# w_out by seven products in batches 1 and 2, squares summed by transfers, and the forms of W held or fetched in smaller pieces

## The chip, the cores and the metric

The kernel runs on one core of a Trainium2 chip. The metric is device time in microseconds of one launch, taken as the median of several runs; lower is better. Engines are named as in the profile: PE (TensorE matmuls), PEld (its weight loads), DVE (VectorE), ACT (ScalarE), POOL (GpSimd) and SP (the queue of SyncE, which only issues transfers here).

## The reference

Channel attention over four batches of 6080 tokens with 256 channels, followed by a feed-forward layer with a squared relu. All arrays are float32.

```python
qn = q / (norm(q, axis=1) + 1e-6); kn = k / (norm(k, axis=1) + 1e-6)   # q, k, v: (4, 6080, 256)
a = softmax(kn.transpose(0, 2, 1) @ qn / tau)                          # 256 x 256 for each batch
x = (v @ a).reshape(24320, 256)
h = maximum(x @ w_in, 0)                                               # w_in: 256 x 2048
out = (h * h) @ w_out                                                  # w_out: 2048 x 256
```

## The kernel before

The kernel folds the attention matrix into w_in: for each batch it makes W = a @ w_in once, so that the feed-forward layer reads v directly. Every float32 product is made of three matmuls on rounded parts (hi by hi, hi by lo, lo by hi). Both products of the layer are done by Strassen-like schemes in which 2 x 2 blocks of the operands take seven block products in place of eight.

The tokens of a batch are cut into 12 blocks: ten of 512 and two of 480. Two blocks of batch 0 come first in a plain way; from block 2 of batch 0 on, work goes by periods. A period k has a batch b, a block n and a group j of 512 hidden units (j = 0 to 3), four periods to a block, 180 in all. The function `period` writes a period's instructions by hand, and the engines keep this order.

In a period PE makes the seven products of v by the forms of W (named A11, S1, S2, A12, S4, S3, A22 in the order of their use; three matmuls by two halves each, 42 in all, 256 columns wide or 240 in the short blocks), and, for the periods one and two back, the products with w_out: `window_A`, `window_S(.., "S1")` and `window_S(.., "S2")`. A group holds two pairs of hidden blocks. A period is called plain (function `plain`) if only its first pair goes by seven products with w_out and the second by eight. A plain period has 39 of these matmuls, of which three (in the S2 window) are twice as wide: 512 columns, 480 in the short blocks. A period that is not plain has 42, all of 256 or 240 columns. Before the change j = 0 and j = 1 are plain in batches 0, 1 and 2, and no period of batch 3 is; j = 2 and 3 are not plain from block 3 of batch 0 on.

After a product ACT and DVE take its sums out of PSUM, square them (relu on DVE in `relu_squares`, or on ACT where `FREE` holds), make sums of the squares (`first_sums`, `third_sum`, `last_sum`) and split them into hi and lo (`hi_A`, `lo_A`, `hi_S`, `lo_S`). Where a period is plain, the sums and the A parts cover one pair in place of two.

Beside this, `attention` works on the next batch, stepped by `side` at five points of a period: one chunk of q and k per period, which costs 12 matmuls for the Gram matrix, a split on ACT and DVE, a square on ACT and the sum of the squares (`add_squares`) into the tile `acc` on DVE. When its 25 chunks are done, the norms, the softmax and W follow, and `late_forms` makes the forms of W and writes them to DRAM (`wf_kept`). From there `load_forms` fetches them for each period again, four transfers of 384 or 512 KB through SP: the early forms (A11, S1, S2) two periods ahead, the late ones (A12, A22, S3, S4) one ahead. SP's queue is in order: a transfer that waits holds up those behind it. POOL's queue carries the loads of v, the sums of the outputs (`combine`, by accumulating transfers) and their stores.

## Time and profile before

| what | value |
|---|---|
| median of 3 runs | 2139.14 us (2138.82 to 2139.2) |
| span of the profiled execution | 2137.0 us, so about 2.1 us of the median lie around it |
| PE busy | 2123.9 us, 99% of the span |
| DVE busy | 1947.1 us, 91% |
| ACT busy | 1818.6 us, 85% |
| products of the periods on PE | from 160 us to 2083 us |

A matmul's record covers its whole way through the array, so records overlap; what a matmul costs is read from the distance between two starts, and a wait of PE from the idle time ahead of a row.

### The profile page before, as it was taken

The page shows a single profiled execution, that of the slowest core. Times are in us where ns is not written, and L with a number is a line of the kernel's source. Part 1 is how long each engine was busy: PE and PEld are TensorE (multiplying, and loading weights), DVE is VectorE, ACT ScalarE, POOL GpSimd, SP SyncE. Part 2 cuts the span into 40 slices and gives each one's busy share as a digit, 9 for nine tenths or more (in the row PEclk, how much of TensorE's full clock was granted, in tenths as well). Part 3 has the DMA queues.
Part 4 walks back from the last instruction along what each step waited for, and adds up shares of the span by engine and source line. Part 5 has one row for each costly group of instructions (what it writes and reads, how often), then busy time and mean ns, then how long its engine had stood idle before and what let it go on. Part 6 is the DMA issues. An engine that isn't in the chain of part 4 may idle for free.

```text
span 2137.0 us, 43905 instructions
## 1 busy us (share of the span) xinstructions
PE 2123.9 (99%) x16990; PEld 2066.1 (97%) x16990; DVE 1947.1 (91%) x2577; ACT 1818.6 (85%) x2708; POOL 403.4 (19%) x506
## 2 busy tenths in 40 slices
PE   9999999999999999999999999999999999999999
PEld 8789999999999999999999999999999999999998
DVE  6898999998999999988999999999899999999993
ACT  5887888888888888878888888878888999999995
POOL 0000121211222121221222121121212122122121
PEclk9999999999999999999999999999999999999999
DMA  9777888889998888788999788887999788788783
GB/s 345 234 232 264 240 255 252 235 239 283 303 297 262 251 251 262 234 241 247 292 303 288 248 255 257 249 234 229 325 322 314 233 241 252 220 247 248 233 256 86
DMA packets 258865, 548.24 MB, mean 257 GB/s; under 512 B 26848, under 2 KB 120672, under 8 KB 258656
## 3 DMA queue, kind: packets, MB, share of 16 engines
q1 hardware_dynamic: 193696, 449.32, 62.3%
q0 software_dynamic: 64960, 96.11, 20.9%
q8 instruction: 134, 2.20, 0.4%
q14 instruction: 75, 0.61, 0.1%
HBM read 431.75 MB, written 64.23 MB: 232 GB/s over the span
## 4 chain that ended last, share of the span: by engine, by line
PE 89%; DVE 6%; ACT 2%; DMA 2%; issue 1%; SPq 0%; DVEq 0%; ACTq 0%
PE ps_o L27 41%; PE ps_c L27 16%; PE ps_h L27 14%; PE ps_b L27 11%; PE gram L27 4%; DVE x L27 2%; PE ps_w L27 2%; PE ps_o_m L27 1%; ACT x L27 1%; DMA wf<-wf_kept 1%; DVE s_lo L27 1%; DVE acc L27 1%; DMA qk<-in_k 1%; DVE A_lo L27 0%; DMA qk<-in_q 0%
## 5 line engine op out<-in xcount | busy, mean ns | idle before, releaser
L27 DVE TENSOR_TENSOR s_lo<-x,s_hi 128x1024 fp32r<-128x1024 f32 (+1 forms) x384 | 464.0, 1208 | 44.4 <-ACT s_hi L27 44.1
L27 PE MATMUL ps_c<-v_hi,wf 128*128 128x256 f32 (+1 forms) x2160 | 466.9, 280 | 4.4 <-DVE x L27 2.2
L27 POOL DMA_DIRECT2D o<-o x225 | 245.4, 1253 | 1102.7 <-ACT o L27 689.7
L27 ACT CAST s_hi<-x 128x1024 fp32r<-128x1024 f32 (+1 forms) x384 | 399.7, 1041 | 37.6 <-DVE x L27 27.9
L27 DVE TENSOR_TENSOR x<-x 128x1024 f32<-128x1024 f32 (+3 forms) x540 | 389.6, 722 | 10.3
L27 PEld LDWEIGHTS ps_c<-v_hi,wf 128*128 128x128 f32 x2160 | 367.4, 188 | 7.8 <-ACT ps_c L27 3.3
L27 ACT ACTIVATE x<-x 128x512 f32<-128x512 f32 (+2 forms) x540 | 350.0, 648 | 21.7 <-DVE x L27 9.2
L27 PE MATMUL ps_b<-v_hi,wf 128*128 128x256 f32 (+1 forms) x1440 | 309.7, 279 | 1.8 <-DVE nx L27 1.1
L27 PE MATMUL ps_h<-v_hi,wf 128*128 128x256 f32 (+1 forms) x1440 | 309.1, 278 | 0.0
L27 PE MATMUL ps_c<-v_lo,wf 128*128 128x256 f32 (+1 forms) x1080 | 300.9, 279 | 0.0
L27 DVE TENSOR_TENSOR A_lo<-x,A_hi 128x1024 fp32r<-128x1024 f32 (+3 forms) x360 | 276.9, 792 | 18.8 <-ACT A_hi L27 15.3
L27 ACT CAST A_hi<-x 128x1024 fp32r<-128x1024 f32 (+3 forms) x360 | 254.4, 707 | 38.4 <-DVE x L27 25.5
L27 PEld LDWEIGHTS ps_b<-v_hi,wf 128*128 128x128 f32 x1440 | 245.2, 188 | 2.3 <-DVE nx L27 1.3
L27 PEld LDWEIGHTS ps_h<-v_hi,wf 128*128 128x128 f32 x1440 | 244.9, 188 | 0.0
L27 ACT COPY x<-ps_c 128x512 f32<-128x512 f32 (+1 forms) x180 | 105.1, 584 | 158.3 <-PE ps_c L27 158.0
L27 PEld LDWEIGHTS ps_c<-v_lo,wf 128*128 128x128 f32 x1080 | 203.2, 188 | 0.1
L27 PE MATMUL ps_b<-v_lo,wf 128*128 128x256 f32 (+1 forms) x720 | 200.6, 279 | 0.0
L27 PE MATMUL ps_h<-v_lo,wf 128*128 128x256 f32 (+1 forms) x720 | 200.4, 278 | 0.0
L27 DVE TENSOR_TENSOR x<-x,ps_h 128x512 f32<-128x512 f32 (+1 forms) x180 | 122.4, 680 | 76.9 <-PE ps_h L27 76.6
L27 PE MATMUL ps_o<-s_hi,wo_hi 128*128 128x256 f32 (+3 forms) x954 | 190.1, 295 | 0.5 <-ACT s_hi L27 0.5
L27 PE MATMUL ps_o<-s_hi,wo_lo 128*128 128x256 f32 (+3 forms) x954 | 190.2, 295 | 0.0
L27 PE MATMUL ps_o<-s_lo,wo_hi 128*128 128x256 f32 (+3 forms) x954 | 190.0, 295 | 0.1
(166 smaller groups left out, 5166.9 us busy)
## 6 DMA issues: line engine op xcount, KB each, us to landing
wf<-wf_kept SPq DMA_DIRECT2D x360, 512.0 KB, 5.3
wf<-wf_kept SPq DMA_DIRECT2D x360, 384.0 KB, 4.9
o<-o POOLq DMA_DIRECT2D x114, 256.0 KB, 5.9
qk<-in_k SPq DMA_DIRECT2D x87, 256.0 KB, 4.3
qk<-in_q SPq DMA_DIRECT2D x87, 256.0 KB, 4.8
v<-in_vT POOLq DMA_DIRECT2D x76, 256.0 KB, 5.1
out_T<-o POOLq DMA_DIRECT2D x152, 128.0 KB, 4.7
o<-o POOLq DMA_DIRECT2D x76, 128.0 KB, 6.2
```

The source lines that it names most:

```text
L27: return lambda *args, **kwargs: self.tc.keep_in_program_order(issue(*args, **kwargs))
```

## The change

1. `FROM`, which says up to which block a group is plain, goes from all of batches 0, 1 and 2 to blocks 0 to 9 (j = 0) and 0 to 8 (j = 1) of batch 0 alone. 53 periods stop being plain: two and three in batch 0, 24 each in batches 1 and 2.
2. In batches 2 and 3 the squares of q and k are added into `acc` by accumulating transfers on POOL's queue, 24 for a batch; the next chunk is then loaded one period later, and the end of the attention waits one period more.
3. The early forms of a group get a tile of their own (`w_own0` to `w_own3`) and are fetched once a batch, 768 KB in one transfer; the late ones come as four transfers of 256 KB through a ring of four tiles, each issued behind the product that frees its slot.
4. `AFTER_FROM` and `V_LAST_FROM` give batches 1 and 2 the order of parts that batch 3 has; `FREE_FROM` moves a relu from DVE to ACT from block 7 of these batches on.

```diff
-                if self.b == 1 and c < HEAD:
+                if self.b > 1 or self.b == 1 and c < HEAD:
                     pool_engine.dma_start(a, sq, accum_op=ALU.add)
                 else:
                     vector.tensor_add(a, a, sq)
...
             g.add_squares(c)
+            c -= b > 1
             if c0 <= c and c + ahead < g.n:
                 load(c + ahead)
...
-    AFTER_FROM = (12, 12, 12, 0)
-    FREE_FROM = (12, 12, 12, 0)
+    AFTER_FROM = (12, 0, 0, 0)
+    FREE_FROM = (12, 7, 7, 0)
...
-    FROM = {0: (12, 12, 12, 0), 1: (12, 12, 12, 0)}
+    FROM = {0: (10, 0, 0, 0), 1: (9, 0, 0, 0)}
...
+    def load_early(k):
+
+        if k >= len(groups):
+            return
+        b, n, j = groups[k]
+        assert (b, j) in forms_kept
+        if k >= GPB and groups[k - GPB][0] == b:
+            WF[k, 0] = WF[k - GPB, 0]
+            return
+        own = own_tile(j, 3 * 2 * 2 * P, F32R, f"wf{k}_own")
+        WF[k, 0] = own.rearrange("p (i r s m) -> p i r s m", i=2, r=2, s=3)
+        nc.sync.dma_start(WF[k, 0].bitcast(F32), wf_early[b, j])
...
+            f = form[0]
+            t = ring_tile([P, 2, 2, P], f"wf{k}_{f}")
+            WF[k, f] = t.rearrange("p i r (s m) -> p i r s m", s=1)
+            nc.sync.dma_start(t.bitcast(F32), wf_later[b, j, f])
...
-        load_forms(k + 2, 0)
+        load_early(k + 2)
...
         product(k, B2, A12, B21)
+        load_late(k + 1, A12)
...
-        steps = V_LAST if b == B - 1 else V_STEPS
+        steps = V_LAST if b >= V_LAST_FROM else V_STEPS
```

The place where the change is widest is the S2 window. On PE, in the period of batch 1, block 3, j = 3, stands the window for j = 1 two periods back (ps_o are the output sums, s_hi and s_lo the parts of the squares, wo and wS the weights and their sums). Before, one of its three terms reads:

```order
L27 MATMUL ps_o_3_1_9313<-s_hi_9412,wS_hi 128x256
L27 MATMUL ps_o_3_1_9313<-s_hi_9412,wo_hi 128x256
L27 MATMUL ps_o_3_0_9283<-s_hi_9412,wo_hi 128x512
L27 MATMUL ps_o_3_0_9283<-s_hi_9412,wo_hi 128x256
L27 MATMUL ps_o_3_1_9313<-s_hi_9412,wo_hi 128x256
```

In the changed kernel two of the three terms of the same window read:

```order
L27 MATMUL ps_o_3_1_9366<-s_hi_9458,wS_hi 128x256
L27 MATMUL ps_o_3_1_9366<-s_hi_9458,wS_odd_hi 128x256
L27 MATMUL ps_o_3_1_9366<-s_hi_9458,wo_hi 128x256 x2
L27 MATMUL ps_o_3_1_9366<-s_hi_9458,wS_lo 128x256
L27 MATMUL ps_o_3_1_9366<-s_hi_9458,wS_odd_lo 128x256
L27 MATMUL ps_o_3_1_9366<-s_hi_9458,wo_lo 128x256 x2
```

Each term has lost its wide matmul here and four of 256 columns are left; the other windows of the group gain what makes the count of matmuls the same. Over the program 123 matmuls of 512 columns have become 256 wide, and 36 of 480 have become 240 wide; the number of matmuls is as before.

On DVE, in the period of batch 1, block 2, j = 2, while chunk 7 of batch 2 is worked on (x are the squares of a period, qk a chunk, v the next block of tokens), before:

```order
L27 TENSOR_TENSOR s_lo_8788<-x_8595,s_hi_8787 128x1024
L27 SCALAR_TENSOR_TENSOR x_8747<-x_8747 128x2x512
L27 TENSOR_TENSOR s_lo_8808<-x_8595,s_hi_8807 128x1024
L27 TENSOR_TENSOR acc_7752<-acc_7752,qk_7_8402 128x1024
L27 TENSOR_TENSOR v_lo_3_8676<-v_3_8241,v_hi_3_8675 128x768
L27 TENSOR_TENSOR A_lo_8839<-x_8747,A_hi_8838 128x2x512
```

and in the changed kernel:

```order
L27 TENSOR_TENSOR s_lo_8829<-x_8640,s_hi_8828 128x1024
L27 SCALAR_TENSOR_TENSOR x_8791<-x_8791 128x2x512
L27 TENSOR_TENSOR s_lo_8854<-x_8640,s_hi_8853 128x1024
L27 TENSOR_TENSOR v_lo_3_8798<-v_3_8349,v_hi_3_8797 128x1024
L27 TENSOR_TENSOR A_lo_8894<-x_8791,A_hi_8893 128x2x512
```

The addition into `acc` has left DVE for POOL's queue, and the parts of v come one step later in the block.

On SP, where batch 1 ends and batch 2 begins (the sums of W for j = 3 of batch 2 are written, and the next periods' forms are fetched), before:

```order
L27 DMA wf_kept_3_0_3_165<-wS_hi_3_14076 256x1x256
L27 DMA wf_kept_3_0_4_166<-wS_hi_3_14076 256x1x256
L27 DMA wf_kept_3_1_3_167<-wS_lo_3_14077 256x1x256
L27 DMA wf_kept_3_1_4_168<-wS_lo_3_14077 256x1x256
L421 DMA qk_1_14224<-in_q 128x512
L983 DMA wf_0_0_14182<-wf_kept_1_0_3_157 128x768
L983 DMA wf_0_1_14184<-wf_kept_1_1_3_159 128x768
```

and in the changed kernel:

```order
L27 DMA wf_early_3_132<-wS_hi_3_14302 128x2x256
L27 DMA wf_later_3_3_183<-wS_hi_3_14302 128x2x128
L27 DMA wf_later_3_2_182<-wS_hi_3_14302 128x2x128
L27 DMA wf_early_3_132<-wS_lo_3_14303 128x2x256
L27 DMA wf_later_3_3_183<-wS_lo_3_14303 128x2x128
L27 DMA wf_later_3_2_182<-wS_lo_3_14303 128x2x128
L1004 DMA wf_own<-wf_early_3_132 128x1536
L1013 DMA wf_1_14405<-wf_later_1_1_173 128x512
```

The fetch of the early forms of j = 3 (`wf_own`) now stands right behind the writes of the same array, and the fetch of A12 for j = 1 (`wf_1`, for the next period) behind it. Before, a fetch of other forms stood there, and that of j = 3 came eight transfers later.

## Rows read from the trace of the kernel before

**Rows 1.** The page: the span, and busy time, share and instructions of PE and DVE.

```profile
span 2137.0 us, 43905 instructions
PE 2123.9 (99%) x16990; PEld 2066.1 (97%) x16990; DVE 1947.1 (91%) x2577; ACT 1818.6 (85%) x2708; POOL 403.4 (19%) x506
```

**Rows 2.** Busy time in four stretches: batch 1 with the attention beside it (12 periods, blocks 3 to 5), batch 1 with W and its forms beside it (20 periods, blocks 7 to 11), the same 20 periods of batch 2, and batch 3 with nothing beside it (20 periods). Columns: stretch, its length, then busy time and instructions of PE, PEld, DVE, ACT and POOL, the granted clock as a share of 2.4 GHz, the share of the DMA engines, and GB/s.

```profile
735.29:871.93 136.64, 136.64 (x1155) 135.85 (x1154) 131.42 (x162) 120.58 (x175) 26.92 (x33) 1.00 0.83 255
915.46:1127.97 212.51, 211.34 (x1752) 207.50 (x1751) 192.73 (x279) 174.91 (x273) 43.04 (x52) 1.00 0.89 271
...
1443.79:1653.97 210.18, 209.54 (x1735) 205.73 (x1734) 191.12 (x269) 174.79 (x274) 44.20 (x55) 1.00 0.94 297
1693.11:1890.57 197.46, 197.46 (x1682) 197.08 (x1682) 186.43 (x231) 184.05 (x282) 39.52 (x50) 1.00 0.79 238
```

**Rows 3.** What PE waited for from 160 us to the end: total us, times, longest us.

```profile
PE ps_c L27 <- DVE x L27: 2.2, 5, 0.9
PE ps_c L27 <- ACT ps_c L27: 2.1, 3, 0.9
PE ps_b L27 <- DVE nx L27: 1.1, 1, 1.1
PE ps_b L27 <- DMA wf<-wf_kept: 0.7, 1, 0.7
```

**Rows 4.** The order of time on PE: start, length of the merged records, operation, count. Two pairs of 512 columns in the plain blocks; the first and the row behind the last of 12 matmuls of 256 columns; the first and the row behind the last of 18 of 240 columns; two pairs of 480 columns.

```profile
100.29 0.63 PE L27 MATMUL ps_h<-v_hi,w_lo 128*128 128x512 f32 x2
100.76 0.63 PE L27 MATMUL ps_o<-s_hi,wo_hi 128*128 128x512 f32 x2
...
788.64 0.28 PE L27 MATMUL ps_o<-s_hi,wS_hi 128*128 128x256 f32 x1
...
790.04 0.28 PE L27 MATMUL ps_b<-v_hi,wf 128*128 128x256 f32 x1
...
1640.15 0.39 PE L27 MATMUL ps_o<-s_hi,wS_hi 128*128 128x240 f32 x2
...
1642.16 0.28 PE L27 MATMUL ps_b<-v_hi,wf 128*128 128x240 f32 x1
...
2087.16 0.60 PE L27 MATMUL ps_h<-v_hi,w_hi 128*128 128x480 f32 x2
2087.59 0.60 PE L27 MATMUL ps_h<-v_lo,w_hi 128*128 128x480 f32 x2
```

**Rows 5.** DVE's groups by shape in the first stretch of Rows 2: count, busy us, mean ns of one, idle time ahead of them and what ended it.

```profile
L27 DVE TENSOR_TENSOR acc<-acc,qk 128x1024 f32<-128x1024 f32 x12 | 14.6, 1219 | 0.0
L27 DVE TENSOR_TENSOR x<-x 128x512 f32<-128x512 f32 x18 | 12.3, 685 | 0.0
L27 DVE SCALAR_TENSOR_TENSOR x<-x 128x1024 f32<-128x1024 f32 x9 | 11.0, 1219 | 0.0
L27 DVE TENSOR_TENSOR A_lo<-x,A_hi 128x512 fp32r<-128x512 f32 x12 | 8.2, 687 | 1.8 <-ACT A_hi L27 1.8
...
L27 DVE TENSOR_TENSOR A_lo<-x,A_hi 128x1024 fp32r<-128x1024 f32 x6 | 7.3, 1222 | 0.2
L27 DVE TENSOR_TENSOR x<-x 128x1024 f32<-128x1024 f32 x6 | 7.3, 1219 | 0.0
...
L27 DVE TENSOR_TENSOR x<-x 128x256 f32<-128x256 f32 x12 | 5.1, 422 | 0.2
```

**Rows 6.** ACT's groups by shape in the same stretch, same columns.

```profile
L27 ACT ACTIVATE x<-x 128x512 f32<-128x512 f32 x30 | 19.0, 634 | 0.8
...
L27 ACT CAST A_hi<-x 128x512 fp32r<-128x512 f32 x13 | 8.1, 625 | 1.7 <-PE ps_c L27 1.5
...
L27 ACT CAST A_hi<-x 128x1024 fp32r<-128x1024 f32 x6 | 6.3, 1052 | 0.0
...
L27 ACT CAST A_hi<-x 128x256 fp32r<-128x256 f32 x6 | 2.4, 407 | 0.2
```

**Rows 7.** What DVE waited for in the second stretch of Rows 2 (915.46 to 1127.97): the largest entry.

```profile
DVE x L27 <- PE ps_h L27: 15.0, 15, 2.4
```

**Rows 8.** The page's transfers: queue, count, KB each, median us from issue to landing.

```profile
wf<-wf_kept SPq DMA_DIRECT2D x360, 512.0 KB, 5.3
...
wf_kept<-wS_lo SPq DMA_DIRECT2D x24, 256.0 KB, 7.5
...
acc<-qk_heads POOLq DMA_DIRECT2D x3, 512.0 KB, 6.1
```

**Rows 9.** In order of time where batch 1 ends and batch 2 begins, start and length: the first matmul of the last period of batch 1 on PE, the last sums of W for batch 2 on DVE, and SP's merged issues.

```profile
1116.13 0.27 PE L27 MATMUL ps_b<-v_hi,wf 128*128 128x240 f32 x1
...
1116.40 1.22 DVE L27 TENSOR_TENSOR wS_lo<-w_sums,wS_hi 128x1024 fp32r<-128x1024 f32 x1
...
1119.63 1.34 SPq L27 DMA_DIRECT2D wf_kept<-wS_hi  x2
1121.01 2.87 SPq L27 DMA_DIRECT2D wf_kept<-wS_lo  x2
...
1124.69 16.47 SPq L983 DMA_DIRECT2D wf<-wf_kept  x10
```

**Rows 10.** DVE and PE in order of time at the norms of batch 2: start, length, count, and the idle time ahead with what ended it.

```profile
924.92 1.80 DVE L27 TENSOR_TENSOR v<-v 128x256 f32<-128x256 f32 x4
...
926.85 0.38 PE L27 MATMUL ps_b<-v_hi,wf 128*128 128x256 f32 x1 [1.11 <-DVE nx L27]
```

More of the change, by code (lines that the diff above doesn't have):

```diff
@@ L163 @@
     wi_kept = [[scratch.tile([P, NC, GRP], F32, name=f"wi_kept{g}_{i}") for i in range(2)] for g in range(NG)]
-    wf_kept = {
-        (b, g, i): [scratch.tile([P, 2, n, P], F32, name=f"wf_kept{b}_{g}_{i}_{n}") for n in (3, 4)]
+    wf_early = {(b, g): scratch.tile([P, 2, 2, 3, P], F32, name=f"wf_early{b}_{g}") for b in range(B) for g in range(NG)}
+    wf_later = {
+        (b, g, f): scratch.tile([P, 2, 2, P], F32, name=f"wf_later{b}_{g}_{f}")
         for b in range(B)
         for g in range(NG)
-        for i in range(2)
+        for f in range(1, 5)
     }
@@ L195, in keep_blocks @@
     def keep_blocks(b, g, i, part, issue):
-        early, later = wf_kept[b, g, i]
-        src = part.bitcast(F32).rearrange("p c (r i m) -> p c r i m", r=2, i=2)
-        for to, c, f in ((early[:, :, 0, :], 0, 0), (later[:, :, 0, :], 1, 0), (later[:, :, 1, :], 1, 1)):
-            issue(to, src[:, c, :, f, :])
+        src = lambda c, f: part(c).bitcast(F32).rearrange("p (r i m) -> p r i m", r=2, i=2)[:, :, f, :]
+        issue(wf_early[b, g][:, i, :, 0, :], src(0, 0))
+        issue(wf_later[b, g, A12[0]][:, i], src(1, 0))
+        issue(wf_later[b, g, A22[0]][:, i], src(1, 1))
     def keep_sums(b, g, i, part, issue):
-        early, later = wf_kept[b, g, i]
         src = part.bitcast(F32).rearrange("p (r s m) -> p r s m", r=2, s=4)
-        issue(early[:, :, 1:3, :], src[:, :, 0:2, :])
-        issue(later[:, :, 2:4, :], src[:, :, 2:4, :])
+        issue(wf_early[b, g][:, i, :, 1:3, :], src[:, :, 0:2, :])
+        for s, form in ((2, S3), (3, S4)):
+            issue(wf_later[b, g, form[0]][:, i], src[:, :, s, :])
+    by_half = lambda tile: lambda c: tile[:, c, :]
+    A11, S1, S2 = ((0, at) for at in range(3))
+    A12, S4, S3, A22 = ((1 + at, 0) for at in range(4))
     wp_kept = [[scratch.tile([P, NC, GRP], F32, name=f"wp_kept{g}_{i}") for i in range(2)] for g in range(NG)]
@@ L325, in forms_of_W @@
         w32, S = room()
-        vector.tensor_add(w32, w_hi.bitcast(F32), w_lo.bitcast(F32))
+        for c in range(NC):
+            vector.tensor_add(w32[:, c, :], w_hi(c).bitcast(F32), w_lo(c).bitcast(F32))
         yield
@@ L329, in forms_of_W @@
             keep_blocks(b, g, i, part, nc.sync.dma_start)
-        if b == B - 1:
-            for kept, part in zip(wp_kept[g], (w_hi, w_lo)):
-                nc.sync.dma_start(kept, part.bitcast(F32))
         w4, S4 = v(w32), S.rearrange("p (r s m) -> p r s m", r=2, s=4)
@@ L362, in late_forms @@
         for i, part in enumerate((w_hi, w_lo)):
-            keep_blocks(b, g, i, part, sync.dma_start)
+            keep_blocks(b, g, i, by_half(part), sync.dma_start)
         if b == B - 1:
@@ L392, with ring_tile, own_tile, W_tiles @@
     OWN_BUFS = {"qk": QK_BUFS, "dec": 1}
-    FAST_TAGS = ("qk",) * QK_BUFS + ("w_lo",) * NG + ("w_hi",) * NG
+    FAST_TAGS = ("qk",) * QK_BUFS + tuple(f"w_own{g}" for g in range(NG)) + ("s1_hi", "s1_lo", "s2_hi", "s2_lo")
+    def ring_tile(shape, name):
+        return wpool.tile(shape, F32R, tag="w_ring", name=name, bufs=4)
+    def own_tile(g, cols, dt, name):
+        return wpool.tile([P, 6, C], dt, tag=f"w_own{g}", name=name, bufs=1).rearrange("p a c -> p (a c)")[:, 0:cols]
+    def W_tiles(b, g):
+        own, more = own_tile(g, 3 * GRP, F32R, f"w{b}_{g}"), ring_tile([P, GRP], f"w_lo{b}_{g}")
+        return (lambda c: own[:, c * GRP : (c + 1) * GRP]), (lambda c: more if c else own[:, 2 * GRP : 3 * GRP])
     class Gram:
@@ L580, in attention @@
         yield
+        if b > 1:
+            yield from until("mid")
+            yield
         yield from until("dve")
@@ L771, in load_v_blocks @@
         half = tn // 2
-        raw = pool.tile([P, 8, half], F32, tag="v", name=f"v{b}_{n}", bufs=1)
+        raw = pool.tile([P, 7, half], F32, tag="v", name=f"v{b}_{n}", bufs=1)
         for slot, c in ((1, 1), (3, 0)):
@@ L861, in first_product @@
             tensor.matmul(
-                ps[:, :tn], wt[:, c, f0 : f0 + P], vt[:, c, :tn], start=i == 0, stop=i == len(parts) - 1
+                ps[:, :tn], wt(c)[:, f0 : f0 + P], vt[:, c, :tn], start=i == 0, stop=i == len(parts) - 1
             )
@@ L999, in two_halves @@
         return ps_h.tile([P, 2, T // 2], F32, tag=tag, name=name)
-    A11, S1, S2 = ((0, at) for at in range(3))
-    A12, A22, S3, S4 = ((1, at) for at in range(4))
     T3, B21, B22, B11, T1, T2, T4 = range(7)
@@ L1013, in product @@
         for p in range(2):
-            late, at = form
-            w_hi, w_lo = (WF[k, late, i][:, p, at, :] for i in range(2))
+            piece, at = form
+            w_hi, w_lo = (WF[k, piece][:, i, p, at, :] for i in range(2))
             for i, (wt, vt) in enumerate(((w_hi, v_hi), (w_hi, v_lo), (w_lo, v_hi))):
@@ L1329, in period @@
         product(k, C, A22, T4)
+        load_late(k + 1, A22)
         evict_C21(k)
@@ L1420 @@
         if i == 26:
-            load_forms(0, 0)
-            load_forms(0, 1)
+            load_early(0)
+            for form in (A12, S4, S3, A22):
+                load_late(0, form)
     for _ in prep:
```

46 lines of the change are left out of this document (22 added, 24 removed).

## The prediction, made before the changed kernel ran

> **What bounds the kernel now.** The page comes first: PE is busy for 2123.9 of the span's 2137.0 us, DVE for 91% [rows 1]. Since matmul records overlap, a busy PE proves little, so the next view is what PE waited for: from 160 us to the end 6.1 us in all, none of it regular [rows 3]. PE then runs its matmuls as closely as it can, and the price of one is the distance between starts: 0.465 us for two of 512 columns, 0.233 each; 12 of 256 columns in 1.40 us, 0.117 each; 18 of 240 in 2.01 us, 0.112 each; 0.43 us for two of 480, 0.215 each [rows 4]. The stretches confirm it: batch 3 has 1682 matmuls in 197.46 us, 0.117 us each [rows 2]. The clock is granted in full, the 2.4 GHz level, in all four stretches, so no term below changes it. The matmuls' columns bound the kernel; DVE is close behind, with 131.42 of 136.64 us (96%) beside the attention and 192.73 of 212.51 (91%) beside W and its forms [rows 2]. What is to be decided is whether fewer columns on PE are paid for by work on DVE, ACT and the queues that now takes the lead.
>
> **PE, removed.** 53 periods stop being plain, and in each three matmuls become half as wide, at an equal count: 123 go from 512 to 256 columns and 36 from 480 to 240. That is 123 x (0.233 - 0.117) = 14.3 us and 36 x (0.215 - 0.112) = 3.7 us [rows 4], **18.0 us** together. All of it lies on the engine that sets the end. Here a rule speaks against the change: the Trainium skill, "TensorE: Matmul & The Clock Gate", section "Back-to-back issue gap", says that in a stream of weight loads and matmuls the spacing is set by both, about 81 ns at 128 columns and 131 ns at 512; read straight between them this is an estimate of 98 ns at 256, 33 ns for a halved width, and 159 x 33 ns = 5 us in place of 18. The rows differ: 233 against 117 ns. Its case stands among the rivals.
>
> **DVE and ACT, added and removed.** A period that stops being plain sums two pairs instead of one. On DVE `first_sums` goes from 512 to 1024 elements (1.219 - 0.685), two further sums from 256 to 512 (2 x (0.685 - 0.422)), the early A parts from 512 to 1024 (1.222 - 0.687) and the late ones from 256 to 512 (about 0.26, from the sums of these sizes): 1.86 us [rows 5]. On ACT `hi_A` adds (1.052 - 0.625) + (0.625 - 0.407) = 0.64 us [rows 6]. Beside the attention of batches 1 and 2 a block of four periods gains 2 x 1.86 = 3.7 us on DVE and loses four additions into `acc`, 4 x 1.22 = 4.9 us [rows 5]. DVE goes from 131.42 / 3 = 43.8 to 42.6 us a block, PE from 45.5 to 45.5 - 6 x 0.116 = 44.8 us [rows 2, 4]: 95% where it was 96%, and there PE waited for nothing. I cost this at 0.
>
> Beside W and its forms there is no addition to lose, and it is tighter. In the 20 periods of batch 1, DVE gains 10 x 1.86 = 18.6 us and loses, by `FREE_FROM`, 15 x (1.219 - 0.685) = 8.0 us [rows 5]: 192.7 becomes 203.3, while PE's length falls from 212.5 by 18 x 0.116 + 12 x 0.103 = 3.3 to 209.2 us, so 97%. ACT gains 10 x 0.64 + 15 x 2 x 0.634 = 25.4 us [rows 6], 174.9 becomes 200.3 us, 96%. What can hide this is DVE's idle time here, 19.8 us, of which 15.0 is DVE being ahead and waiting for PE's sums [rows 7]; that part vanishes by itself when DVE falls behind. Batch 3 runs DVE at 94% and ACT at 93% with PE busy throughout [rows 2]. Some peaks will show: I take 0.5 us for each of the two stretches, **1 us**, from 0 (the cover holds) to 4 each (half of the 8 us a stretch that the idle rate of the first stretch, 5.2 us in 12 periods, would leave).
>
> **The squares by transfer.** 48 transfers of 512 KB onto POOL's queue. Such a transfer lands in 6.1 us [rows 8]. It is issued near the end of a period; the load that needs its slot stands on SP behind the next period's S3 product, 48 matmuls or 5.6 us in, and behind that load stands the fetch of A22, which anyway waits until PE has used A22, near 9.8 us. So in a usual period nothing queued on SP is held up; in the period in which POOL first stores four outputs and loads v it may be issued up to 4 us late, and still lands before 9.8 us. The chunk itself is loaded a period ahead of its use. Cost 0.
>
> **The forms.** Per period 1 MB is fetched in place of 1.8, so the DMA engines, busy at 0.79 to 0.94 [rows 2], get freer: no cost. But each fetch of early forms at the start of a batch stands on SP's queue behind the writes of W's sums, and in four places straight behind the writes of the very array it reads: for j = 2 and 3 of batch 1, j = 3 of batch 2, j = 3 of batch 3. SP then waits until the write has landed, and behind it waits the fetch of A12 for the next period. Worked at the place in rows 9: the period's first matmul starts at 1116.13, the sums are there at 1117.62 (1.5 us in), and the lo writes went out at 1121.01 (4.9 us in). A write lands after 7.5 us, a fetch after 5.3 us [rows 8], with some 0.4 us between the two issues. So A12 is there between 1.5 + 7.5 + 0.4 + 5.3 = 14.7 and 18.1 us after the period's start. PE wants it at 84 x 0.117 + 30 x 0.117 = 13.3 us. PE waits 1.4 to 4.8 us in each place; if a write lands early, nothing. That SP is slow after such writes is seen there too: the next ten fetches went out over 16.5 us [rows 9]. Since the slots ahead on SP come free earlier now, I take 1.5 us, near the low end: four places, **6 us**, from 0 to 19.
>
> **The order of batch 3.** `AFTER_FROM` and `V_LAST_FROM` move the late A parts behind the next period's first copy on ACT, and the parts of v, with the load of the next block on POOL, one step later, behind the stores of the outputs. Batch 3 runs in this order with PE busy all the time [rows 2], so it costs 0; if the load of v came late instead, DVE's four subtractions (1.8 us, [rows 10]) would, once a block.
>
> **Waits that go.** Of the 6.1 us [rows 3], the fetch (0.7) stands at one of these places and is replaced. The norms of batch 2 made PE wait 1.1 us, behind four subtractions for v on DVE [rows 10]; they now come one period later, away from these. The five waits of ps_c for DVE come where the window between S3 and A22 is short, and it now has nine matmuls (1.05 us) more in j = 0 and 1: I take 0.5 off. Together **2.3 us** less, bounds 0 to 4.
>
> **Sum.** The span of 2137.0 and 2.1 us around it give 2139.1, the median of the runs. 2139.1 - 18.0 + 1 + 6 - 2.3 = **2125.8 us**, 0.6% faster.
>
> **Rivals.**
> (a) The queue takes it back: at the four places PE waits the full 4.8 us, 19 us, and the late fetches behind A12 nothing more. 2139.1 - 18.0 + 19 - 1 = 2139 us, no change. For it speaks that the lo writes went out 4.9 us in [rows 9]; against it, that the writes stood behind other fetches then. Chance 9%, with all mixtures that end within 0.2%.
> (b) VectorE becomes the bound beside W and its forms. If DVE keeps the idle time it has there, 19.8 us, its stretch takes 203.3 + 19.8 = 223 us in place of 209.2, 14 us more, and 28 in both: 2139.1 - 18.0 + 28 = 2149 us, slower. It costs from 209.2 - 203.3 = 5.9 us of idle time in a stretch on, and decides against the change from 5.9 + 9.0 = 15 us on. Against it: three quarters of that idle time was waiting for PE [rows 7], and at 96% busy in the first stretch DVE was idle for only 0.44 us a period (8.7 us in 20) [rows 2], which would cost 3 us. Chance 6%.
> (c) Width hardly counts, because the weight loads set the spacing: a halved matmul gains nothing, and the time is 2139.1 + 1 + 6 - 2.3 = 2144 us at no gain at all. The rows speak against it with 0.233 and 0.117 us at an equal weight load [rows 4]. By the rule of the Trainium skill named above the gain would be an estimate of 5 us and the time 2139. Chance 1%.
> (d) The queue's waits don't show, since the writes land sooner than PE gets there: 2139.1 - 18.0 + 1 - 2.3 = 2119.8 us. Chance 25%.
> That the change doesn't do what it says can be left aside: the counts of matmuls by width, of additions on DVE and of transfers on POOL are read from the instructions.
>
> **How the numbers follow.** The forecast, with waits between the extremes, has 59%, (d) 25%, (a) 9%, (b) 6%, (c) 1%. The range leaves out half of the upper cases and the best corner: from 2118.5 (18.0 and 2.6 us gained, no new wait) to 2135 (15 us of new waits). About 0.2%, 4.3 us, is what a measurement of this kernel can tell from no change: faster than 2134.9 has 59 + 25 = 84%, between the bounds 10%, slower 6%.
>
> **What would show it.** Right: the stretch of batches 1 and 2 beside the attention is 0.7 us a block shorter, PE stays without regular waits, POOL shows 48 more `acc` transfers and DVE 48 fewer additions; PE's waits name `wf` fetches in four places, of one to three us each. Wrong: waits of PE for DVE `x` or ACT in blocks 7 to 11 of batches 1 and 2 that come back every block (b); waits for `wf` of over 4 us, or a wait in every period, which would mean that the fetches through the ring come too late or that SP is held up by an `acc` transfer; or equal starts for wide and narrow matmuls (c).

## The result and the profile after

The changed kernel takes **2152.94 us**, the median of 4 runs (2150.94 to 2154.26), against 2138.98 us (2137.38 to 2139.20, 4 runs) of the kernel before in the same measurement: a ratio of 1.0067 (95% interval 1.0052 to 1.0081). It is 14 us slower, not 13 us faster. The profiled execution took 2152.09 us, its span 2150.3.

The page after, beside [rows 1]: the span, and busy time, share and instructions of the engines.

```profile
span 2150.3 us, 44660 instructions
...
PE 2119.6 (99%) x16990; PEld 2061.0 (96%) x16990; DVE 1974.8 (92%) x2533; ACT 1870.6 (87%) x2768; POOL 432.9 (20%) x554
...
PE 72%; DVE 15%; ACT 8%; DMA 3%; issue 2%; SPq 1%; DVEq 0%; ACTq 0%
```

PE is busy for 4.3 us less than before in a span that is 13.3 us longer. The last line is the chain of the work that ended last: 72% of it is on PE, where it was 89% before. Since records overlap, "99% busy" is no sign that all is well; what PE waited for from 160 us to the end, as in [rows 3], shows the trouble:

```profile
PE ps_c L27 <- ACT ps_c L27: 9.6, 15, 1.5
PE ps_c L27 <- DVE x L27: 7.9, 10, 2.0
PE ps_b L27 <- DMA wf<-wf_later: 2.8, 3, 1.1
PE ps_c L27 <- DMA wf<-wf_later: 2.2, 1, 2.2
PE ps_b L27 <- DVE nx L27: 0.9, 2, 0.6
PE gram L27 <- DVE qk_lo L27: 0.4, 1, 0.4
```

That is 23.8 us in place of 6.1. Only 5.0 us of it is fetches; 17.5 us is ACT's copy of `ps_b` into `ps_c` and DVE's `x`. The list is not the whole loss: 18.0 us of columns gone and 14 us more time make some 32 us of new delay, and the list grew by 17.7. It holds only idle time between records, and a start that is late by less than the records overlap leaves none; two stretches at the lower clock (last section) are some 3 us more.

The windows say where. Each is cut at ACT's copy of `ps_b` into `ps_c` in its first period, which is itself late where ACT is, so lengths are good to less than a us. First the changed kernel: batch 0 (40 periods), block 0 of batch 1 (4), then the four stretches of [rows 2], cut at the same periods, with block 0 of batch 2 in the fifth row. Then the kernel before, for the three stretches that [rows 2] lacks.

```profile
158.58:609.15 450.57, 441.56 (x3622) 431.23 (x3621) 421.57 (x591) 374.67 (x566) 80.77 (x102) 1.00 0.68 195
609.15:654.28 45.13, 42.35 (x355) 41.34 (x353) 41.35 (x49) 36.63 (x55) 8.48 (x11) 1.00 0.75 221
744.35:879.47 135.12, 135.12 (x1155) 134.71 (x1154) 128.93 (x151) 122.75 (x175) 35.87 (x45) 1.00 0.89 234
922.47:1138.15 215.68, 211.21 (x1753) 207.55 (x1752) 202.51 (x280) 194.47 (x303) 41.25 (x54) 0.99 0.73 207
1138.15:1186.07 47.92, 44.64 (x364) 44.00 (x363) 41.20 (x49) 38.12 (x57) 10.69 (x15) 0.96 0.78 217
1453.07:1666.80 213.73, 209.49 (x1748) 205.39 (x1747) 203.14 (x280) 194.08 (x304) 40.28 (x51) 1.00 0.77 227
1706.26:1903.72 197.46, 197.46 (x1682) 197.08 (x1682) 186.43 (x231) 183.99 (x282) 42.43 (x55) 1.00 0.60 159
```

```profile
159.35:602.05 442.70, 439.06 (x3617) 430.58 (x3616) 414.02 (x591) 371.18 (x567) 80.97 (x100) 1.00 0.85 262
602.05:644.20 42.15, 41.73 (x353) 41.26 (x352) 37.82 (x49) 36.22 (x55) 8.93 (x11) 1.00 0.91 284
...
1127.97:1173.14 45.17, 44.44 (x377) 43.98 (x376) 40.59 (x51) 39.08 (x59) 11.26 (x15) 1.00 0.92 291
```

Against before, batch 0 is 7.9 us longer, the first blocks of batches 1 and 2 are 3.0 and 2.8, and the two stretches beside W 3.2 and 3.6 us longer, where 3.3 us fewer columns should have made them shorter. Beside the attention it is 1.5 us shorter in 12 periods, with PE never idle, and batch 3 is the same to 0.01 us. So the columns are gained where nothing else is tight, and the loss lies in batch 0, at the starts of the batches and beside W.

### The profile page after: what moved, and what is told of

Same layout as the page of the kernel before. It is cut to its first block, busy times and chain, and to the rows that moved or that the text cites. A ratio compares the mean times of both kernels' runs of the same rounds, so it can differ in the third digit from the quotient of the medians.

```text
span 2150.3 us, 44660 instructions
## 1 busy us (share of the span) xinstructions
PE 2119.6 (99%) x16990; PEld 2061.0 (96%) x16990; DVE 1974.8 (92%) x2533; ACT 1870.6 (87%) x2768; POOL 432.9 (20%) x554
## 4 chain that ended last, share of the span: by engine, by line
PE 72%; DVE 15%; ACT 8%; DMA 3%; issue 2%; SPq 1%; DVEq 0%; ACTq 0%
PE ps_o L27 32%; PE ps_c L27 14%; PE ps_h L27 11%; PE ps_b L27 9%; DVE x L27 5%; PE gram L27 3%; ACT x L27 3%; DVE s_lo L27 2%; DVE A_lo L27 2%; PE ps_w L27 1%; ACT s_hi L27 1%; DMA wf<-wf_later 1%; DVE v_lo L27 1%; ACT A_hi L27 1%; PE ps_o_m L27 1%
## 5 line engine op out<-in xcount | busy, mean ns | idle before, releaser
L27 DVE TENSOR_TENSOR x<-x 128x1024 f32<-128x1024 f32 (+2 forms) x540 | 445.9, 826 | 19.1 <-ACT x L27 0.8
L27 DVE TENSOR_TENSOR A_lo<-x,A_hi 128x1024 fp32r<-128x1024 f32 (+2 forms) x360 | 324.5, 908 | 24.2 <-ACT A_hi L27 21.4
L27 ACT CAST A_hi<-x 128x1024 fp32r<-128x1024 f32 (+2 forms) x360 | 286.4, 796 | 44.9 <-DVE x L27 38.8
L27 PE MATMUL ps_c<-v_hi,wf 128*128 128x256 f32 (+1 forms) x1440 | 313.4, 281 | 10.3 <-DVE x L27 7.9
L27 PE MATMUL ps_c<-v_hi,wf_own 128*128 128x256 f32 (+1 forms) x720 | 158.8, 284 | 9.9 <-ACT ps_c L27 9.6
L27 DVE SCALAR_TENSOR_TENSOR x<-x 128x512 f32<-128x512 f32 (+3 forms) x180 | 160.7, 893 | 0.0
L27 PE MATMUL ps_b<-v_hi,wf 128*128 128x256 f32 (+1 forms) x720 | 155.1, 279 | 2.8 <-DMA wf<-wf_later 2.8
L27 PE MATMUL ps_b<-v_hi,wf_own 128*128 128x256 f32 (+1 forms) x720 | 155.1, 279 | 0.9 <-DVE nx L27 0.9
L27 PE MATMUL ps_h<-v_hi,wf 128*128 128x256 f32 (+1 forms) x720 | 155.0, 279 | 0.0
L27 PE MATMUL ps_h<-v_hi,wf_own 128*128 128x256 f32 (+1 forms) x720 | 154.6, 279 | 0.0
L27 PE MATMUL ps_o<-s_hi,wo_lo 128*128 128x256 f32 (+2 forms) x689 | 153.7, 293 | 0.0
```

The costliest lines, as they stand in the source:

```text
L27: return lambda *args, **kwargs: self.tc.keep_in_program_order(issue(*args, **kwargs))
```

## Experiments

"Before" in each is the kernel before, run on the same chip. Unless another count is given, a median is over 4 runs.

### One part of the changed kernel undone

`plain_again`: j = 0 and 1 of batches 0 to 2 plain again, with the two tables that came with the seven products (`AFTER_FROM`, `FREE_FROM`); `seven_attn`: seven products in j = 0 and 1 only beside the attention (blocks 0 to 5 of batches 1 and 2) and in batch 3; `sq_dve`: squares on VectorE; `v_steps`: the steps of v of batches 0 to 2 as before.

```diff
# plain_again
-    AFTER_FROM = (12, 0, 0, 0)
-    FREE_FROM = (12, 7, 7, 0)
+    AFTER_FROM = (12, 12, 12, 0)
+    FREE_FROM = (12, 12, 12, 0)
...
-    FROM = {0: (10, 0, 0, 0), 1: (9, 0, 0, 0)}
+    FROM = {0: (12, 12, 12, 0), 1: (12, 12, 12, 0)}
# v_steps
-    V_LAST_FROM = 0
+    V_LAST_FROM = B - 1
# seven_attn
-    FREE_FROM = (12, 7, 7, 0)
+    FREE_FROM = (12, 12, 12, 0)
...
-        return (b, n) == order[OLD] if j in EARLY else n < FROM[j][b]
+        return (b, n) == order[OLD] if j in EARLY else b == 0 or b < B - 1 and n >= 6
# sq_dve
-                if self.b > 1 or self.b == 1 and c < HEAD:
+                if self.b == 1 and c < HEAD:
...
-            c -= b > 1
...
-        if b > 1:
-            yield from until("mid")
-            yield
```

> The changed kernel with batches 0, 1 and 2 plain again in j = 0 and 1 (FROM, AFTER_FROM and FREE_FROM as before); squares by transfer, the forms in SBUF and the order of v's parts stay. PE gets its 18.0 us of columns back. Theory P (the sums of the second pair make VectorE and ScalarE late beside W): about 15 us of PE's waits go, so 2153 + 18 - 15 = 2156 us or a little less, with waits left only for fetched forms and in batch 0. Theory Q (the waits come from the transfers and the order of v's parts, not from the second pair): they all stay, and the time is 2153 + 18 = 2171 us.

> The changed kernel with V_LAST_FROM = 3, so that batches 0 to 2 take the parts of v in their old steps. Theory V (v's second lo part, 0.95 us on VectorE ahead of the sums at the start of j = 3, makes ScalarE's next copy late): the waits of ps_c for ScalarE at j = 0 of batch 0, blocks 4 to 6 (1.5, 0.5, 0.5 us) go, and some of those beside W: 2143 to 2148 us. Theory P: the order matters little against the added sums, 2151 to 2154 us.

> The changed kernel with seven products throughout only in blocks 0 to 5 of batches 1 and 2, beside the attention; from block 6 on, and in batch 0, j = 0 and 1 are plain, and FREE_FROM is as before. 24 periods with 0.348 us less: 8.4 us of columns saved of the 18.0. Theory P: the waits beside W go back to those before the change, save the fetches (6 us) and what the order of v's parts costs (some 7 us): 2139 - 8.4 + 13 = 2144 us. Theory Q: all 31 us of new waits stay, 2139 - 8.4 + 31 = 2162 us.

> The changed kernel with the squares of batches 2 and 3 added on VectorE again, chunks loaded and the end of the attention timed as before. Theory P with VectorE as the next bound: a block beside the attention asks 42.6 + 4.9 = 47.5 us of VectorE where PE needs 45.0, so 2.5 to 4 us more in each of 12 blocks: 2183 to 2200 us. Theory A (the transfers into acc or the period by which they delay the norms and W cause the new waits): the waits at the ends of batches 1 and 2 shrink, and the time falls below 2153 us.

Measured, with before at 2138.67 us (7 runs): plain_again 2161.39 (ratio 1.0104, 1.0087 to 1.0121), v_steps 2147.84 (1.0043, 1.0028 to 1.0058), seven_attn 2154.01 (1.0069, 1.0053 to 1.0084), sq_dve 2186.61 (1.0225, 1.0209 to 1.0240).

The first and the third run were to tell theories P and Q apart, and both results lie between them: without the seven products, 22.7 us of loss are left, so the loss is not in them alone; and the products gain 8.5 us of their 18, so they lose something too. The transfers are needed: with the squares on VectorE the kernel takes 34 us more, as theory P had it. The clean one is `v_steps`, 5.1 us faster for one line, within the range of theory V. Its windows over the same periods (batch 0, then the two stretches beside W) put 4.6 us of it in batch 0, 445.94 in place of 450.57 us. Elsewhere gains and losses cancel in these two profiles: the stretch of batch 2 beside W is 3.4 us longer, and block 0 of batch 2 is 2.9 us shorter (45.01 us).

```profile
159.71:605.65 445.94, 439.22 (x3617) 430.23 (x3616) 422.00 (x591) 374.13 (x567) 80.58 (x100) 1.00 0.69 196
917.24:1132.58 215.34, 209.39 (x1750) 205.53 (x1749) 202.29 (x279) 194.96 (x302) 42.89 (x55) 1.00 0.73 209
1443.73:1660.89 217.16, 210.26 (x1745) 205.21 (x1744) 203.51 (x280) 194.72 (x304) 41.80 (x54) 1.00 0.77 225
```

How a step on DVE makes PE wait is seen at 243 us of the changed kernel, DVE, ACT and PE in order of time:

```profile
243.02 0.96 DVE L27 TENSOR_TENSOR v_lo<-v,v_hi 128x768 fp32r<-128x768 f32 x1
243.89 0.69 DVE L27 TENSOR_TENSOR x<-x,ps_h 128x512 f32<-128x512 f32 x1
```

```profile
244.62 1.30 ACT L27 ACTIVATE x<-x 128x512 f32<-128x512 f32 x2 [1.66 <-DVE x L27]
...
251.93 0.58 ACT L27 COPY ps_c<-ps_b 128x512 f32<-128x512 f32 x1
```

```profile
252.56 0.39 PE L27 MATMUL ps_c<-v_hi,wf_own 128*128 128x256 f32 x1 [1.51 <-ACT ps_c L27]
```

`V_LAST` puts `v_lo` at the start of j = 3, ahead of `x += ps_h`. ACT, whose relu needs that `x`, stands idle for 1.66 us, then works without a gap for 7 us, and is late with the copy that PE needs. In `v_steps` the `v_lo` runs earlier (at 238.20), ACT idles 0.79 us there, and PE waits 0.86.

### One part alone, on the kernel before

`sq_only`: only the squares by transfers (the three edits of `sq_dve`, the other way round). `forms_only`: only the forms in SBUF, with the ring and the smaller tile for v that the change brings along. `seven_old_forms`: `sq_only` and the seven products (the three tables of `plain_again`, the other way round). `seven_old_attn`: `sq_only` and the seven products beside the attention.

> The kernel before with one part of the change alone: the squares of batches 2 and 3 are summed by transfers, with the loads one chunk and the end of the sum one period later. All periods of j = 0, 1 stay plain, the four fetches a period and the steps of v as before. Two theories of the 22.7 us that the parts without the seven products cost together (2161.4 against 2138.7 us): Q, the forms kept in SBUF and fetched one by one behind the writes of W cause them; S, the transfers do (loads one step later, the end of the sum one period later, POOL's queue). Q: 2137 to 2141 us, VectorE's share of the span down by about 2 points, PE's waits as before (6 us). S: 2146 us or more, with waits of PE for gram or for the norms nx.

> The kernel before with the other part alone: early forms stay in SBUF, later ones come one by one through the ring of four; squares added on VectorE, plain periods and the steps of v as before. Q: 2148 to 2158 us, the waits at the fetches of wf_later (about 5 us) and in the blocks beside W, where the copies on ACT come late. S: 2136 to 2142 us.

> Seven products (FROM, AFTER_FROM, FREE_FROM of the change) and squares by transfers, on the kernel before's four fetches a period and its steps of v. PE has 18 us fewer columns. Q: the scheme of the forms was the costly part, so most of the 18 us shows: 2122 to 2132 us, the rest in waits of PE for DVE x and ACT beside W. S, or a third theory V, that the seven products beside W use up what they save (waits for DVE and ACT of 15 us or more in blocks 9 to 11 of batch 0 and 7 to 11 of batches 1 and 2): 2136 to 2146 us.

> As the run with the old fetches, but seven products only where the attention runs beside (blocks 0 to 5 of batches 1 and 2, j = 0, 1, and batch 3); beside W and in batch 0 all periods of j = 0, 1 stay plain. 24 periods fewer are plain, 72 matmuls x 0.116 us = 8.4 us fewer columns. Q: 2129 to 2134 us. V: the same 2129 to 2134 us and then below the run with seven products throughout. S: 2140 us or more.

Measured, before at 2138.81 us (7 runs): sq_only 2168.35 (1.0141, 1.0124 to 1.0158), forms_only 2148.99 (1.0049, 1.0034 to 1.0064), seven_old_forms 2182.42 (1.0205, 1.0174 to 1.0236), seven_old_attn 2170.84 (1.0151, 1.0136 to 1.0166).

Neither Q nor S holds alone: each part costs something by itself, the transfers 29.5 us (as S had it, not Q) and the forms 10.2 (within Q's range). On the old fetches the seven products add 14.1 us to the price of the transfers (2182.4 against 2168.4, with runs that lie 17 us apart), and 2.5 where they stay beside the attention, which is within the runs' spread. The first is 36 us above every time expected of it; the second is as far above the ranges of Q and V and fits S alone (2140 us or more). That the first takes 11.6 us more than the second, with fewer columns, bears one half of theory V out: beside W the products don't pay. The trace of `sq_only` shows why the transfers cost so much, in three views: the stretch of blocks 3 to 5 of batch 1, the transfers' median time from issue to landing between 640 and 930 us, and what SP waited for in that time.

```profile
735.10:883.45 148.35, 141.42 (x1155) 139.22 (x1154) 119.61 (x150) 121.38 (x176) 36.69 (x45) 0.98 0.94 273
```

```profile
wf<-wf_kept SPq DMA_DIRECT2D x48, 512.0 KB, 7.4
acc<-qk POOLq DMA_DIRECT2D x22, 512.0 KB, 8.6
```

```profile
SPq L27 <- DMA acc<-qk: 139.0, 19, 11.8
```

DVE has 11.8 us less to do than in [rows 2] and the stretch is 11.7 us longer. The DMA engines are busy at 0.94 (0.83 before); a transfer into `acc` takes 8.6 us; SP stands before the next load of q and k for it, up to 11.8 us, with the fetches of forms behind. PE's waits for fetches come to 8.6 us in the whole run, 0.7 before, and its waits for ACT ahead of `ps_c` to 14.3, 2.1 before. In the changed kernel the fetches are smaller and each has another place on SP; the same views read:

```profile
wf<-wf_later SPq DMA_DIRECT2D x104, 256.0 KB, 4.0
acc<-qk POOLq DMA_DIRECT2D x22, 512.0 KB, 6.8
```

```profile
SPq L27 <- DMA acc<-qk: 3.7, 4, 1.9
```

So the two parts should not add up, which the next run tests.

### Both parts together, the place of the early fetch, the relu

`plain_v_steps`: `plain_again` and `v_steps` together. The other three are `v_steps` with the early fetch last; `early_last_attn` also has the two edits of `seven_attn`, `early_last_dve` also `FREE_FROM` of before.

```diff
-        load_early(k + 2)
         late_step()
...
         load_late(k + 1, A22)
+        load_early(k + 2)
         evict_C21(k)
...
-        nc.sync.dma_start(WF[k, 0].bitcast(F32), wf_early[b, j])
+        sync.dma_start(WF[k, 0].bitcast(F32), wf_early[b, j])
```

> The changed kernel with all periods of j = 0, 1 plain again and the steps of v as before: the forms in SBUF and the squares by transfers together, without the seven products. Alone they cost 10.2 us (2149.0 against 2138.8) and 29.6 us (2168.4). Theory A, they add up: 2178 us. Theory B, the transfers cost what they cost only because the DMA engines were full, and the 0.8 MB a period that the forms' scheme no longer fetches makes room for them: what is left is the forms' own price at SP's queue, 2146 to 2156 us, with no wait of SP for acc of several microseconds and none of ACT for the output's store beside the attention.

> The changed kernel with the steps of v as before and the fetch of early forms issued in program order behind the last fetch of the ring in its period, not ahead of the first. Theory F (SP stands in the fetch that waits for the write of its own array): PE's waits for wf_later go (6 us in the run with the steps of v alone) and no wait for wf_own takes their place: 2139 to 2143 us. Rival: the write is late by itself and the ring's fetches wait for writes of their own, so the waits stay or move to wf_own: 2146 to 2150 us.

> As early_last, with the seven products only beside the attention of batches 1 and 2 (blocks 0 to 5) and in batch 3, and the halved relu as before. Theory V (beside W, seven products use up in waits for ACT's copies and DVE's x what they save): 72 matmuls x 0.116 = 8.4 us of columns less than before, no waits beyond before's but some 2 to 4 us at the fetches, 2131 to 2136 us, below both kernels. Rival: the seven products beside W still pay, and this run is not below early_last.

> As early_last, with the relu of blocks 7 to 11 of batches 1 and 2 left on VectorE (FREE_FROM of before). If ACT is the late engine beside W (PE waits for the copy ps_c from ps_b, 12 us in the run with the steps of v alone), less work on ACT makes it faster than early_last by 2 to 6 us; if VectorE is, it is slower, by up to 15 x 0.53 = 8 us, with waits for DVE x in place of those for ACT.

Measured, before at 2137.71 us (13 runs): plain_v_steps 2147.30 (1.0044, 1.0029 to 1.0059), early_last 2148.85 (1.0051, 1.0034 to 1.0068), early_last_attn 2143.91 (10 runs; 1.0030, 1.0021 to 1.0040), early_last_dve 2156.59 (1.0088, 1.0073 to 1.0104).

Theory B holds: forms and transfers together cost 9.6 us, no more than the forms alone. Whether that is the bytes that are no longer fetched or the new places of the fetches on SP was not taken apart. Theory F fell: PE still waited 3.6 us for `wf_later` (5.9 in `v_steps`) and 4.7 us for `wf_own<-wf_early`, the longest 2.6, and the time stayed. The relu back on VectorE costs 7.7 us, with PE's waits for DVE's `x` at 11.1 us in place of 4.1: DVE has no room beside W. With the products kept to the attention (early_last_attn) the time is 4.9 us less, though 8 us above the range expected. And `plain_v_steps` against `v_steps` gives the seven products with their two tables by themselves: 18 us fewer columns and 0.5 us more time, so **they bring 18.5 us of new delay**. PE's lists name 13.2 us of it (23.5 against 10.3), of which 12.8 are ACT's copy and DVE's `x`. The windows of `plain_v_steps`, batch 0 and the two stretches beside W, to be held against the three rows of `v_steps` above:

```profile
158.23:601.77 443.54, 439.46 (x3617) 430.79 (x3616) 414.13 (x591) 371.10 (x566) 81.42 (x101) 1.00 0.69 196
918.08:1131.59 213.51, 212.15 (x1754) 208.01 (x1753) 192.86 (x279) 174.89 (x274) 45.58 (x56) 1.00 0.75 210
1446.15:1658.47 212.32, 210.92 (x1743) 206.75 (x1742) 192.93 (x279) 174.95 (x273) 44.03 (x54) 1.00 0.79 230
```

The products make the stretches beside W 1.8 and 4.8 us longer with 3.3 us fewer columns each, so 5.1 and 8.1 us of delay; batch 0, with five periods more (1.6 us of columns), is 2.4 us longer (443.54 to 445.94), so 4.0 us. In the two stretches beside W, PE's waits for ACT's copy and DVE's `x` are 4.8 and 4.6 us in `v_steps`, 0.8 and none in `plain_v_steps`. DVE is at 94%, ACT at 90%: the mean is not full. A peak is. ACT in `v_steps`, in the period 1056.83 to 1070.53 (11.74 us long in `plain_v_steps`) and at the start of the next, and PE behind it:

```profile
1061.33 1.00 ACT L27 CAST s_hi<-x 128x960 fp32r<-128x960 f32 x1 [1.30 <-DVE x L27]
1062.23 0.56 ACT L27 ACTIVATE x<-ps_b 128x480 f32<-128x480 f32 x1
1062.69 1.01 ACT L27 COPY o<-ps_o 128x1024 f32<-128x1024 f32 x1
1063.58 1.25 ACT L27 ACTIVATE x<-x 128x480 f32<-128x480 f32 x2
1064.74 0.98 ACT L27 CAST s_hi<-x 128x960 fp32r<-128x960 f32 x1
1065.63 0.60 ACT L27 ACTIVATE x<-x 128x480 f32<-128x480 f32 x1
1066.13 0.67 ACT L27 ACTIVATE w<-ps_w,rinv 128x512 f32<-128x512 f32 x1
1066.70 1.03 ACT L27 CAST wS_hi<-w_sums 128x1024 fp32r<-128x1024 f32 x1
1067.64 1.00 ACT L27 CAST v_hi<-v 128x960 fp32r<-128x960 f32 x1
1068.53 0.99 ACT L27 CAST A_hi<-x 128x960 fp32r<-128x960 f32 x1
...
1070.53 0.55 ACT L27 COPY ps_c<-ps_b 128x480 f32<-128x480 f32 x1
```

```profile
1071.14 0.38 PE L27 MATMUL ps_c<-v_hi,wf_own 128*128 128x240 f32 x1 [1.63 <-ACT ps_c L27]
```

W's eviction, the hi part of its sums, that of v, the copy of an output and the larger relus and A parts all fall into one period; ACT, held up first by DVE's `x` for 1.3 us, has no gap for 9 us, and the copy goes out with PE already waiting, 1.6 us in all. This is one such period, read closely; that the others are alike is an inference from the waits.

### The order on ACT, and the queue of the writes

`attn_v_steps`: `v_steps` with the two edits of `seven_attn`. `attn_pool_writes`: the same, with the writes of forms on POOL's queue; `attn_pool_last`: that, with the early fetch last. `v_steps_a_first`: `v_steps` with `AFTER_FROM` of before.

```diff
# attn_pool_writes
-            keep_blocks(b, g, i, by_half(part), sync.dma_start)
+            keep_blocks(b, g, i, by_half(part), pool_engine.dma_start)
-            keep_sums(b, g, i, part, sync.dma_start)
+            keep_sums(b, g, i, part, pool_engine.dma_start)
# v_steps_a_first
-    AFTER_FROM = (12, 0, 0, 0)
+    AFTER_FROM = (12, 12, 12, 0)
```

> The changed kernel with the steps of v as before and the seven products only beside the attention of batches 1 and 2 and in batch 3; the fetch of early forms where the change has it. Against early_last_attn (2143.9 us) it gives the price of the place of that fetch alone. If the place matters, 2145 to 2149 us; if it only moves the wait, 2141 to 2144 us.

> As attn_v_steps, with the twelve writes of a group's forms issued on POOL's queue, not on SP's. Theory I (SP's issue of the writes, some 0.6 us each and two bursts of six, holds the fetches behind them): the waits for wf_later fall below 2 us in all, 2133 to 2139 us. Theory L (the fetches wait until the writes have landed): the waits stay, 2141 us or more; if the writes land later behind the stores of the outputs on POOL, slower still.

> As attn_pool_writes, with the fetch of early forms behind the last fetch of the ring in its period. Theory I: 2132 to 2137 us, below the kernel before and the lowest of all, since nothing is left on SP ahead of the ring's fetches. Theory L: waits for wf_own at the first period of a form, 2141 us or more.

> The changed kernel with the steps of v as before and the late A parts of batches 1 and 2 where they were before, ahead of the next period's first copy on ACT (AFTER_FROM). If the late copy on ACT is a matter of the work ahead of it, 0.4 to 0.6 us more stand ahead of it and the waits for ps_c from ACT (11.8 us) grow, 2150 to 2158 us; if it is ACT's load, the time stays at 2148 us.

Measured, before at 2138.62 us (13 runs): attn_v_steps 2141.34 (10 runs; 1.0017, 1.0007 to 1.0026), attn_pool_writes 2162.03 (1.0110, 1.0095 to 1.0125), attn_pool_last 2147.91 (1.0045, 1.0030 to 1.0060), v_steps_a_first 2166.00 (1.0133, 1.0118 to 1.0148).

With the late A parts ahead of the copy again, PE's waits for it are (all of `v_steps_a_first`):

```profile
PE ps_c L27 <- ACT ps_c L27: 24.9, 37, 2.8
```

in place of 11.8 us in 17 times, and the kernel is 18 us slower, more than expected: what stands ahead of the copy on ACT decides. Theory I fell: with the writes on POOL's queue PE waits longer for fetches (7.0 and 5.1 us at the starts of batches 2 and 3), and ACT's copy comes later too. With the writes on SP the place of the early fetch, 2143.9 against 2141.3 us, is worth little, as expected if it only moves the wait. With the writes on POOL it is worth 14 us (2162.0 against 2147.9): SP then stands in the early fetches for 29.4 us until the sums of W have landed, and with these fetches last PE's waits for `wf_later` fall from 12.8 to 4.3 us, with 2.8 for `wf_own` added.

`attn_v_steps` also says by runs where the products pay. Against `plain_v_steps` it is 6.0 us faster, for 8.4 us of columns beside the attention. `v_steps` has the other 9.6 us of columns gone too, beside W and in batch 0, and a relu moved to ACT for it, and is 6.5 us slower than `attn_v_steps`: 16 of the 18.5 us of delay belong there.

### The writes in two halves

`attn_split`: `attn_v_steps` with the writes of the hi halves a quarter of a period earlier (for the sums alike); `attn_split7`: also seven products in block 6.

```diff
         vector.tensor_sub(w_lo, w32, w_hi.bitcast(F32))
+        keep_blocks(b, g, 0, by_half(w_hi), sync.dma_start)
         yield from until("dve")
-        for i, part in enumerate((w_hi, w_lo)):
-            keep_blocks(b, g, i, by_half(part), sync.dma_start)
+        keep_blocks(b, g, 1, by_half(w_lo), sync.dma_start)
# attn_split7
-        return (b, n) == order[OLD] if j in EARLY else b == 0 or b < B - 1 and n >= 6
+        return (b, n) == order[OLD] if j in EARLY else b == 0 or b < B - 1 and n >= 7
```

> As attn_v_steps, with the six writes of the hi halves of a group's forms issued at the point mid, a quarter of a period ahead of those of the lo halves; the bytes and the queue are the same. Theory L (the fetches that open a batch wait for the landing of the forms just written): writes that go out 2 to 3 us earlier take that much off each of the two long waits for wf_later (2.7 and 1.7 us), 2136 to 2139 us. Rival: only the last write, of the lo half, counts, and it goes out no earlier: 2140 to 2143 us.

> As attn_split, with the seven products also in block 6 of batches 1 and 2, 12 matmuls x 0.116 us = 1.4 us of columns less. If the end of the attention can carry them, 1 to 1.5 us below attn_split; if its norms and the first sums for W already fill DVE and ACT, the same or slower.

Measured, before at 2138.24 us (19 runs): attn_split 2142.12 (9 runs; 1.0020, 1.0010 to 1.0030), attn_split7 2141.24 (11 runs; 1.0015, 1.0007 to 1.0024). The rival's time came: writing the hi halves earlier gains nothing. Block 6 by seven products gives 0.9 us where 1 to 1.5 were expected, less than the runs differ among themselves. No version here beats the kernel before; the nearest is within 0.2% of it.

## Why the prediction was wrong, step by step

The medians make a chain from before to after: 2138.7, with forms and transfers 2147.3 (+9 us), with the seven products 2147.8 (18 us of columns gone, 18.5 us of delay come), with the steps of v 2152.9 (+5). In another order the shares differ: the steps of v cost 14.1 us where the periods are plain (2161.4 against 2147.3) and 12.7 where the products stay beside the attention (2154.0 against 2141.3), so the products after them gain 8.5 us.

- **Columns, 18.0 us: right.** The stretch beside the attention shows it: 134.70 us in `v_steps` and 135.12 in the changed kernel, in place of 136.64 for three blocks, so 0.65 and 0.5 us a block where 0.7 was said. Rival (c), that width hardly counts, falls with it.
- **Peaks beside W, 1 us, from 0 to 8: the step that failed.** They are 13 us in the two stretches and 4 more in batch 0, which the prediction did not look at. The loads came out near what was worked out (DVE 202.5 where 203.3 was said, ACT 194.5 where 200.3), and DVE's wait for PE's sums fell from 15.0 to 5.4 us, as foretold. What failed is the argument from means: that batch 3 runs at 94% on DVE and 93% on ACT without a wait. There every block has the same work in the same order; beside W a period can hold W's eviction, its sums, the parts of v and an output at once and the next none of them, and PE can't run ahead, since ACT copies into `ps_c` between two of its products. Rival (b) named the place and put the price at 14 us a stretch; it was 5 to 8, and more of PE's waits there are for ACT's copy (3.2 and 3.4 us in `v_steps`) than for DVE's `x` (1.6 and 1.2), the engine that the rival named.
- **The order of batch 3, 0: failed by 5 us.** Batch 3 had this order before and runs the same (197.46 us). But `V_LAST_FROM = 0` moves the steps of v in batch 0 as well, which the list of the change, naming batches 1 and 2, leaves out, and 4.6 us of the 5 are there: VectorE still adds squares in batch 0, and the moved `v_lo` stands ahead of a sum that ACT waits for. In the other two pairs of runs that differ only in this line batch 0 loses as much (448.59 against 443.54 us, 448.53 against 442.93); what the line costs outside batch 0 was not followed up. The late A parts, costed at 0 with it, are no cost but what makes the products bearable.
- **The queue, 6 us: the mechanism right, the price in part by luck.** SP stood where the prediction said, in the fetch of the early forms until the write of their sums had landed, at all four places:

```profile
SPq L1004 <- DMA wf_early<-wS_lo: 9.8, 4, 4.8
```

Behind two of them, j = 3 of batches 1 and 2, PE waited for A12, 1.14 us (ending at 633.06) and 1.04 (at 1154.51), and behind the other two not at all: 2.2 us in place of 6. The reason is the terms taken for a landing: such a write landed in 3.5 us and a fetch from `wf_later` in 3.5 (medians), where 7.5 and 5.3 had been used. PE's list still comes to 5.0 us because of two other waits, 0.62 us in the second stretch beside W and this one, which the prediction did not have:

```profile
1137.65 0.33 SPq L435 DMA_DIRECT2D qk<-in_k  x1
...
1138.57 0.37 SPq L1013 DMA_DIRECT2D wf<-wf_later  x1
...
1146.12 0.35 PE L27 MATMUL ps_c<-v_hi,wf 128*128 128x256 f32 x1 [2.22 <-DMA wf<-wf_later]
```

The fetch of A22 stood on SP behind a load of k and q, which had waited 6.7 us for DVE's sums of W (`wS_lo`). And the whole scheme of the forms costs 9 to 10 us by the runs, more than PE's waits for fetches. Other places for the early fetch, for the writes or for half of them each left the price or raised it, so no run here took it away; that PE pays for the landing of a form that is written and read back fits these, but was not shown by itself.

- **The squares by transfer, 0, and fewer bytes, "no cost": right, but only together.** The transfers cost 29.5 us beside the old fetches and nothing beside the new ones. The prediction treated the new scheme of fetches as a side effect here; it is what makes room for the transfers.
- **Waits that go, 2.3 us: hardly.** PE's waits for DVE's `x` grew from 2.2 to 7.9 us, and the norms still cost PE 0.9 us, 1.1 before.

Open: how the forms' 9 to 10 us divide between landing, clock, order and the smaller tile for v, why the steps of v cost more in plain kernels, and whether less work on ACT beside W (rather than work moved between ACT and DVE) would set the products free.

## What to carry to other kernels

A mean load, even one compared with a stretch that runs at the same mean, says nothing of peaks: lay the added instructions into the worst period, on the engine whose result PE reads next, and count what stands ahead of that result. When a table changes for all batches, cost it in each stretch, not only in the one it was made for. A sum of waits that comes out near the forecast is checked place by place: here more than half of it stood where the forecast had not looked. And undo parts in pairs: one part cost 30 us alone and nothing beside the other.
